# A first layer in 26 block products instead of seven, in a retention and feed-forward kernel on one core

## The chip, the cores and the metric

The kernel runs on one NeuronCore of a Trainium2 chip. The metric is the device time of one execution in microseconds (us). Before the change two runs took 679.41 and 679.5 us, median 679.45; the profiled execution spans 677.6 us.

The engines have short names in the profile: PE is TensorE (matrix products), PEld its weight loads, DVE is VectorE, ACT is ScalarE, POOL is GpSimd, SP is SyncE. PSUM is the memory into which TensorE writes, in eight banks; SBUF is the working memory.

## The reference, cut to what matters

A retention block feeds a feed-forward block. Shapes: batch 4, 8 heads, 768 positions, head size 64; so 3072 tokens of 512 numbers go into the second block, whose inner width is 2048. All is fp32.

```python
for t in range(S):
    state = gamma * state + einsum('bhd,bhe->bhde', k[:, :, t], v[:, :, t])
    y[:, :, t] = scale * einsum('bhd,bhde->bhe', q[:, :, t], state)
x = y.transpose(0, 2, 1, 3).reshape(3072, 512)

h = x @ w_in                                   # 512 -> 2048, the first layer
sp = maximum(h, 0) + log1p(exp(-abs(h)))       # softplus
g = h * erf(sp)                                # the gate
out = g @ w_out                                # 2048 -> 512, the second layer
```

## The kernel before

The first 512 tokens go through both layers by ordinary products, in four groups of inner columns, while VectorE converts the weights from 64-bit words. The other 2560 tokens go in ten chunks of 256. Each chunk is two "later groups", one for each half of the 2048 inner columns, so there are 20 later groups; I number them 0 to 19. In each, both layers are computed as seven block products in place of eight (Strassen's scheme in Winograd's form), and beside them one visit (`sub_visit`) advances the retention for a later chunk of 128 positions. There are 18 visits; the last two groups have none.

Engines run their own instructions in program order. A tile pool with `bufs=2` hands out two buffers in turn; a product into a bank has to wait until the last reader of that bank is done.

```python
ps_r = ctx.enter_context(tc.tile_pool(name="ps_r", bufs=2, space=PSUM))   # two banks
ps_h = ctx.enter_context(tc.tile_pool(name="ps_h", bufs=2, space=PSUM))   # two banks
ps_o = ctx.enter_context(tc.tile_pool(name="ps_o", bufs=1, space=PSUM))   # four banks, for the output

def sums(which, s):                  # sums of weight blocks, on VectorE, 1024 wide
    ...
    for to, a, b, plus in of:        # four for "in", four for "out", for each half s
        nc.vector.tensor_tensor(x[to], x[a], x[b], op=ALU.add if plus else ALU.subtract)
        yield

def x_sums(g):                       # sums of token blocks, once a chunk
    xs = ret.tile([P, 4, 2, P], F32, name="xs", bufs=1)
    ...
    for to, a, b in ((t1, b12, b11), (t2, b22, t1), (t3, b22, b12), (t4, b21, t2)):
        nc.vector.tensor_tensor(to, a, b, op=ALU.subtract)

def hidden_part(g, p):               # one of the seven products of the first layer
    if p == 1:
        HS[g] = act.tile([P, N], F32, name="h")
        BK[g] = [ps_h.tile([P, FG, P], F32, name="hp") for _ in range(2)]
    ...
    for u in range(FG):              # 4 x 2 = 8 matmuls of 128x128 by 128x128
        for kk in range(2):
            nc.tensor.matmul(bank[:, u, :], w_in_sb[:, s, IN[a], kk, u * P : (u + 1) * P],
                             XS[m][b][:, kk, :], ...)
    flat = bank.rearrange("p u t -> p (u t)")
    # the bank is read 512 wide: by ScalarE for p = 1, 6, 7, 4, by VectorE (added) for 2, 3, and once more for 7

def gate(g):                         # softplus and erf on ScalarE, 2048 wide
def gated(g):                        # e = h * e on VectorE, two operations of 1024
def g_sums(g):                       # four sums of blocks of g, 512 wide, on VectorE
def project_part(g, p, ...):         # one of the seven products of the second layer, 4 matmuls
    ...
    if b[0] == "T":
        need("sums out", s)          # draws weight sums until those it needs are there
    ...
    next(last_steps, None)           # draws one more step of the weight sums
def put_part(m, step):               # adds up the output and stores it, four steps

def sub_visit(j, g):
    pp = [ret_psum() for _ in range(2)]                  # both banks of ps_r
    def of_state(a):
        for u in PAIRS:
            for r in range(2):
                nc.tensor.matmul(pp[r][...], x[own, u, :], QT[j][own, u, t], ...)
    other = SC[j + 1] = [ret_psum(ps_h) for _ in range(2)]   # both banks of ps_h
    if c:
        of_state(0)
    ...

for g in range(G0, NG):              # the later groups
    hidden_part(g, 1); hidden_part(g, 2)
    ...                              # put_part of the chunk before, in every second group
    hidden_part(g, 6)
    for _ in range(2):
        next(last_steps, None)
    if not first:
        g_sums(g - 1)
    hidden_part(g, 5); hidden_part(g, 7)
    for _ in range(2):
        next(last_steps, None)
    project_part(g - 1, 1)           # in the first later group: project(g - 1, 0)
    hidden_part(g, 4); hidden_part(g, 3)
    if more: sub_visit(j, g)
    if g + 1 < NG and (g - G0) % 2: x_sums(g + 1)
    K_(j + 2); T(j + 2)              # scaling (3 operations) and transposes (2) on VectorE
    project_part(g - 1, 2); project_part(g - 1, 4)
    gate(g)
    for p in (5, 6, 7, 3): project_part(g - 1, p)
    gated(g)
```

Of the kernel before, what the change touches and what calls it, by code (L numbers as in the profile page):

```python
# [19 lines left out]
P = 128  # L20
C = 128
# [11 lines left out]
IN = {"11": 0, "12": 1, "21": 2, "22": 3, "S3": 2, "S1": 4, "S2": 5, "S4": 6}  # L33
# [6 lines left out]


# [4 lines left out]
def kernel(  # L46
# [84 lines left out]
    w_in_sb = const.tile([P, 2, 7, 2, FG * P], F32, name="w_in_sb")  # L131
    w_out_sb = const.tile([P, 2, 7, FG, DH], F32, name="w_out_sb")

    def w_in_of(ft, kk):
        half, s, i = ft // (2 * FG), ft % (2 * FG) // FG, ft % FG
        return w_in_sb[:, s, 2 * half + kk // 2, kk % 2, i * P : (i + 1) * P]

    def w_out_of(ft):
# [6 lines left out]
    spare = [  # L145
        x[:, s, 4:7].rearrange("p a b c -> p (a b c)") for s, x in
        ((0, w_out_sb), (1, w_out_sb), (1, w_in_sb), (0, w_in_sb))
    ]
    raws = [x[:, : 2 * CE].bitcast(I64) for x in spare]
    numbers = spare[0][:, 2 * CE :].bitcast(U32)  # L150
    powers = [x[:, 2 * CE :].bitcast(U32) for x in spare[1:3]]
# [38 lines left out]
    def conversion(n):  # L190
# [8 lines left out]
            range(2) if n < 4 else (None,), (slice(2), slice(2, 4)) if n == 0 else (slice(None),)  # L199
        )  # L200
        for part, rows in parts:
            last = n > 0 or rows.start == 2
            words = raws[place[n]].bitcast(U32)
            if which == "in":
                f = slice(at * 2 * P, (at + 1) * 2 * P)
                if part is not None:
                    f = slice((at * 2 + part) * P, (at * 2 + part + 1) * P)
                to = w_in_sb[:, s, 2 * half : 2 * half + 2, :, f].rearrange("p d k f -> p (d k) f")
            else:
                to = w_out_sb[:, s, 2 * half : 2 * half + 2, at * 2 : at * 2 + 2, :].rearrange(  # L210
                    "p d f c -> p d (f c)"
                )
            words = words.rearrange("p (a b w) -> p a b w", a=to.shape[1], w=2)
            number, power = (
                x.rearrange("p (a b) -> p a b", a=to.shape[1]) for x in (numbers, powers[n % 2])
            )
            if part is not None:
                f = slice(part * P, (part + 1) * P)
                words, number, power = words[:, rows, f], number[:, rows, f], power[:, rows, f]
                to = to[:, rows]  # L220
            lo, hi = words[:, :, :, 0], words[:, :, :, 1]
# [24 lines left out]

    def sums(which, s):

        if which == "in":
            assert all(("hidden", 2 * FG + s * FG + u) in done for u in range(FG))  # L250
            x = {name: w_in_sb[:, s, at] for name, at in IN.items()}
            of = (("S1", "21", "22", 1), ("S2", "S1", "11", 0), ("S3", "11", "21", 0), ("S4", "12", "S2", 0))
        else:
            assert ("project", s) in done
            x = {name: w_out_sb[:, s, at] for name, at in OUT.items()}
            of = (("T1", "12", "11", 0), ("T2", "22", "T1", 0), ("T3", "22", "12", 0), ("T4", "21", "T2", 0))
        for to, a, b, plus in of:
            nc.vector.tensor_tensor(x[to], x[a], x[b], op=ALU.add if plus else ALU.subtract)
            yield
        done.add(("sums " + which, s))  # L260
# [76 lines left out]
    state_1, state_2 = (const.tile([P, HP, D], F32, name=f"state{i}") for i in range(1, 3))  # L337
# [479 lines left out]
    XS, BK = {}, {}  # L817
# [6 lines left out]
    def x_quarter(m, dh, th):  # L824
        at = m % 2 * SCH + th * P
        return XC[m // 2][:, 2 * dh : 2 * dh + 2, at : at + P]

    def x_sums(g):

        m = chunk_of(g)  # L830
        xs = ret.tile([P, 4, 2, P], F32, name="xs", bufs=1)
        b11, b12, b21, b22 = (x_quarter(m, d, t) for d in range(2) for t in range(2))
        t1, t2, t3, t4 = (xs[:, i] for i in range(4))
        for to, a, b in ((t1, b12, b11), (t2, b22, t1), (t3, b22, b12), (t4, b21, t2)):
            nc.vector.tensor_tensor(to, a, b, op=ALU.subtract)
        XS[m] = {"11": b11, "21": b21, "22": b22, "T1": t1, "T2": t2, "T3": t3, "T4": t4}

    def hidden_part(g, p):


        m, s = chunk_of(g), (g - G0) % 2
        if p == 1:
            HS[g] = act.tile([P, N], F32, name="h")
            BK[g] = [ps_h.tile([P, FG, P], F32, name="hp") for _ in range(2)]
        h = {name: HS[g][:, i * TCH : (i + 1) * TCH] for name, i in HQ.items()}
        a, b = PRODUCTS[p]
        if a[0] == "S":
            need("sums in", s)
        bank = BK[g][0 if p in (1, 6, 7, 4) else 1]
        for u in range(FG):  # L850
            for kk in range(2):
                nc.tensor.matmul(  # L852
                    bank[:, u, :],
                    w_in_sb[:, s, IN[a], kk, u * P : (u + 1) * P],
                    XS[m][b][:, kk, :],
                    start=(p in (1, 2, 5) and u == 0 and kk == 0),
                    stop=True,
                    skip_group_check=True,
                )
        pace(1.5)  # L860
        flat = bank.rearrange("p u t -> p (u t)")
        if p == 1:
            nc.scalar.copy(h["11"], flat)
        elif p == 2:
            nc.vector.tensor_tensor(h["11"], h["11"], flat, op=ALU.add)  # L865
            pace(-0.6)
        elif p == 6:
            nc.scalar.copy(h["12"], flat)  # L868
        elif p == 7:
            nc.scalar.copy(h["22"], flat)  # L870
            other = BK[g][1].rearrange("p u t -> p (u t)")
            nc.vector.tensor_tensor(h["22"], h["22"], other, op=ALU.add)  # L872
            pace(-0.6)
        elif p == 4:
            nc.scalar.copy(h["21"], flat)  # L875
        elif p == 3:
            nc.vector.tensor_tensor(h["12"], h["12"], flat, op=ALU.add)  # L877
            pace(-0.6)
# [18 lines left out]
    def g_sums(g):  # L897
# [4 lines left out]
        for i in range(4):  # L902
            x[f"S{i + 1}"] = HS[g][:, i * TCH : (i + 1) * TCH]
        for to, a, b, plus in (
# [3 lines left out]
        G[g] = x  # L908
        pace(-2.4)
# [161 lines left out]

    j = JPC + 2
    put = None
    for g in range(G0, NG):
        first = g == G0
        more = j < NJ
        hidden_part(g, 1)
        hidden_part(g, 2)
        if first:
            gated(g - 1)  # L1080
        if put is not None:
            for step in range(3):
                put_part(put, step)
        hidden_part(g, 6)
# [3 lines left out]
        for _ in range(2):  # L1088
            next(last_steps, None)
        if put is not None:  # L1090
            put_part(put, 3)
            put = None
        if not first:
            g_sums(g - 1)
        hidden_part(g, 5)
        hidden_part(g, 7)
        for _ in range(2):
            next(last_steps, None)
        if first:
            K_(j + 1)  # L1100
            T(j + 1)
            project(g - 1, 0)
# [93 lines left out]
```

## Time and profile before

| | before |
|---|---|
| time, median of two runs | 679.45 us |
| span of the profiled execution | 677.6 us |
| TensorE matmuls, busy | 671.8 us, 6400 records |
| VectorE, busy | 392.1 us |
| ScalarE, busy | 257.0 us |
| first layer of the later groups (line 852) | 2240 records, 149.7 + 113.7 us |
| second layer of the later groups (line 924) | 1128 records, 142.0 + 112.1 us |
| granted TensorE clock | 1.000 |

How to read it: the page of the profile gives for each engine the time in which it was busy and its share of the span. A matmul of the source in fp32 shows as two records, so 20 groups of 56 matmuls are 2240 records. Records of matmuls overlap and their ends are modelled, so the distance from one start to the next tells more than the length of one record. In the lists, "h<-h,hp 128x512" means that a 512-wide operation wrote tile h from tiles h and hp; "[3.99 <-PE hp L852]" means that its engine stood idle for 3.99 us before it and that a matmul of line 852 ended the wait. V is used below for the moment at which a visit ends on TensorE.

### The profile page before, as it was taken

How to read it: one execution, taken by the hardware profiler on the slowest of the kernel's cores; microseconds unless marked ns; L12 is line 12 of the kernel's file. 1: busy time of each engine (PE TensorE's matmuls, PEld its weight loads, DVE VectorE, ACT ScalarE, POOL GpSimd, SP SyncE). 2: the span in 40 equal slices, each digit the busy share in tenths (PEclk: the TensorE clock that was granted, in tenths of full speed). 3: DMA queues.
4: the chain of work that ended last, by engine and by line, in shares of the span. 5: the costliest groups of instructions: out<-in, count | busy, mean ns of one | idle time of the engine just before them, and what ended most of it. 6: DMA issues, size and time to landing. Idle time of an engine off the chain costs nothing.

```text
span 677.6 us, 14849 instructions
## 1 busy us (share of the span) xinstructions
PE 671.8 (99%) x6400; PEld 575.4 (85%) x6400; DVE 392.1 (58%) x635; ACT 257.0 (38%) x294; POOL 7.4 (1%) x20
## 2 busy tenths in 40 slices
PE   8999999999999999999999999999999999999998
PEld 7744444668999999999999999999999999999997
DVE  5999999667845445634644553554554544333324
ACT  3477453333414415334144143242341441432430
POOL 1000000200000000000000000000000000000000
PEclk9999999999999999999999999999999999999999
DMA  9999753333423112312322321222222300000000
GB/s 188 231 254 256 178 144 77 59 61 62 119 48 75 34 32 47 76 36 43 76 41 38 76 46 31 64 44 47 69 40 45 74 2 1 1 33 1 1 32 31
DMA packets 156721, 47.67 MB, mean 70 GB/s; under 512 B 143088, under 2 KB 147568, under 8 KB 156656
## 3 DMA queue, kind: packets, MB, share of 16 engines
q1 hardware_dynamic: 156240, 46.72, 31.6%
q8 instruction: 50, 0.82, 0.5%
q14 instruction: 15, 0.12, 0.1%
q10 hardware_dynamic: 416, 0.01, 0.0%
HBM read 40.39 MB, written 6.29 MB: 69 GB/s over the span
## 4 chain that ended last, share of the span: by engine, by line
PE 98%; DMA 1%; DVE 0%; SPq 0%; ACT 0%; issue 0%
PE hp L852 37%; PE o L924 36%; PE hp L759 8%; PE o L795 8%; PE r L638 2%; PE hp L530 1%; PE o L674 1%; DMA kq<-in_k_dram 1%; PE hp L653 1%; PE r L459 1%; PE r L653 1%; PE o L506 1%; PE r L446 1%; PE r L674 0%; PE o L515 0%; PE o L499 0%
## 5 line engine op out<-in xcount | busy, mean ns | idle before, releaser
L852 PE MATMUL hp<-xs,w_in_sb 128*128 128x128 f32 x1280 | 149.7, 275 | 0.0
L852 PEld LDWEIGHTS hp<-xs,w_in_sb 128*128 128x128 f32 x1280 | 147.8, 192 | 1.5 <-issue 0.5
L924 PE MATMUL o<-w_out_sb,h 128*128 128x256 f32 (+1 forms) x648 | 142.0, 377 | 0.4 <-DVE r L1151 0.4
L924 PEld LDWEIGHTS o<-w_out_sb,h 128*128 128x128 f32 x648 | 122.3, 190 | 16.8 <-DVE r L1151 0.6
L852 PE MATMUL hp<-xT,w_in_sb 128*128 128x128 f32 x960 | 113.7, 275 | 0.0
L852 PEld LDWEIGHTS hp<-xT,w_in_sb 128*128 128x128 f32 x960 | 112.0, 192 | 1.9 <-issue 1.0
L924 PE MATMUL o<-w_out_sb,e 128*128 128x256 f32 x480 | 112.1, 383 | 0.0
L748 DVE TENSOR_TENSOR e<-h,e 128x1024 f32<-128x1024 f32 x42 | 49.5, 1221 | 100.0 <-ACT e L729 100.0
L924 PEld LDWEIGHTS o<-w_out_sb,e 128*128 128x128 f32 x480 | 88.3, 190 | 11.4
L759 PE MATMUL hp<-xT,w_in_sb 128*128 128x512 f32 (+2 forms) x144 | 56.5, 548 | 0.0
L877 DVE TENSOR_TENSOR h<-h,hp 128x512 f32<-128x512 f32 x20 | 13.8, 688 | 72.3 <-PE hp L852 72.3
L719 ACT ACT_TABLE_LOAD x24 | 30.8, 1283 | 60.8 <-issue 45.4
L759 PEld LDWEIGHTS hp<-xT,w_in_sb 128*128 128x128 f32 x144 | 25.8, 190 | 26.9 <-issue 24.6
L729 ACT ACTIVATE e<-e 128x2048 f32<-128x2048 f32 (+1 forms) x23 | 42.1, 1836 | 0.2
L719 ACT ACTIVATE e<-h 128x2048 f32<-128x2048 f32 x22 | 42.0, 1910 | 0.2
L865 DVE TENSOR_TENSOR h<-h,hp 128x512 f32<-128x512 f32 x20 | 13.7, 687 | 37.5 <-PE hp L852 37.5
L870 ACT COPY h<-hp 128x512 f32<-128x512 f32 x20 | 11.7, 586 | 61.0 <-PE hp L852 61.0
L875 ACT COPY h<-hp 128x512 f32<-128x512 f32 x20 | 11.7, 585 | 60.3 <-PE hp L852 60.3
L868 ACT COPY h<-hp 128x512 f32<-128x512 f32 x20 | 11.7, 585 | 57.1 <-PE hp L852 57.1
L692 ACT COPY xT<-r 128x256 f32<-128x256 f32 x33 | 10.8, 375 | 57.9 <-PE r L638 57.9
L729 ACT ACT_TABLE_LOAD x24 | 30.8, 1283 | 0.4
L872 DVE TENSOR_TENSOR h<-h,hp 128x512 f32<-128x512 f32 x20 | 13.8, 688 | 27.8 <-ACT h L870 27.8
(144 smaller groups left out, 667.8 us busy)
## 6 DMA issues: line engine op xcount, KB each, us to landing
w_out_sb<-in_moe_w_out_dram SPq DMA_DIRECT2D x14, 512.0 KB, 5.5
kq<-in_k_dram SPq DMA_DIRECT2D x23, 256.0 KB, 3.9
v<-in_v_dram SPq DMA_DIRECT2D x23, 256.0 KB, 3.2
out_dram<-r SPq DMA_DIRECT2D x23, 256.0 KB, 2.7
kq<-in_q_dram SPq DMA_DIRECT2D x288, 16.0 KB, 1.8
kb<-in_k_dram SPq DMA_DIRECT2D x288, 16.0 KB, 1.7
w_in_sb<-in_moe_w_in_dram SPq DMA_DIRECT2D x8, 512.0 KB, 9.5
w_in_sb<-in_moe_w_in_dram SPq DMA_DIRECT2D x8, 256.0 KB, 7.7
```

Of the source, the lines that this page charges most:

```text
L638: nc.tensor.matmul(pp[r][col * D : (col + 1) * D, u % 2, t], x[own, u, :], QT[j][own, u, t], start=first(r, col), stop=True, skip_group_ch ...
L653: nc.tensor.matmul(other[a][own, u % 2, D:] if crossed else pp[a][own, u % 2, t], V[j][t, 2 * u + r, :], AM[j][t, r, u, :D], start=crossed ...
L719: nc.scalar.activation(E[g], HS[g], AF.Softplus)
L729: nc.scalar.activation(E[g][:, half], E[g][:, half], AF.Erf)
L748: nc.vector.tensor_tensor(E[g][:, half], HS[g][:, half], E[g][:, half], op=ALU.mult)
L759: nc.tensor.matmul(HP_[ft][:, t], w_in_of(ft, kk), XC[0][:, kk, t], start=(kk == 0), stop=(kk == n_k - 1),)
L795: nc.tensor.matmul(O[0][tt].rearrange("p (d c) -> p d c", d=2), E[g][:, u * TCH + tt * P : u * TCH + (tt + 1) * P], w_out_of(ft), start=(f ...
L852: nc.tensor.matmul(bank[:, u, :], w_in_sb[:, s, IN[a], kk, u * P : (u + 1) * P], XS[m][b][:, kk, :], start=(p in (1, 2, 5) and u == 0 and ...
L865: nc.vector.tensor_tensor(h["11"], h["11"], flat, op=ALU.add)
L872: nc.vector.tensor_tensor(h["22"], h["22"], other, op=ALU.add)
L877: nc.vector.tensor_tensor(h["12"], h["12"], flat, op=ALU.add)
L924: nc.tensor.matmul(O[m][i][:, half, at], G[g][a][:, u * P : (u + 1) * P], w_out_sb[:, s, OUT[b], u, at], start=i not in started, stop=(s = ...
```

## The change

The first layer of the later groups is split finer. For each half of the inner columns the weights are cut into 4 x 4 blocks (four blocks of 128 inputs, four of 256 inner columns), the tokens into two blocks of 128. By the ordinary scheme this takes 32 products of one weight block with one token block, by seven 2x2x2 products the equal of 28; a table in the new kernel gives 26. Each takes two matmuls. What it is for: fewer matmuls on TensorE.

Each product is a step: it is added into one of four banks (two of ps_h, two of ps_r), and the running content of the bank is then read into, or added to or taken from, one or two of the eight output blocks, each 256 wide. The first write of a block is ScalarE's, the others VectorE's. The sums of blocks that the products need are 30 of weights (256 wide, for each half) and 18 of tokens (128 wide, for each chunk), most of them in place. Three projection parts of the second layer move in between the steps.

The diff, cut to its core:

```diff
+N_W, N_X = 26, 18
+W_SUMS = (
+    (16, 2, 6, "+"),
+    (2, 2, 3, "+"),
 ... 30 entries: to, a, b, sign
+X_SUMS = (
+    (0, (1, 0), (1, 1), "-"),
 ... 18 entries
+STEPS = (                    # weight block, token block, bank, new chain, reads
+    (20, 5, 0, True, ((1, False),)),
+    (21, (1, 0), 1, True, ((4, True),)),
 ... banks of steps 1 to 26: 0 1 2 3 0 1 0 1 2 3 0 1 2 3 0 1 1 1 0 2 3 1 1 0 1 3
+    (7, 13, 0, False, ((2, True),)),              # step 15
 ...
+    (13, (2, 0), 3, False, ((6, True),)),         # step 26
+)
-    w_in_sb = const.tile([P, 2, 7, 2, FG * P], F32, name="w_in_sb")
+    w_in_sb = const.tile([P, 2, N_W, 2 * P], F32, name="w_in_sb")
 ... the conversion of the weights follows the new layout
+    def sum_in(s, upto):
+        while in_sums[s] < upto:
+            to, a, b, sign = (x if i == 3 else w_in_sb[:, s, x] for i, x in enumerate(W_SUMS[in_sums[s]]))
+            nc.vector.tensor_tensor(to, a, b, op=OP[sign])
+            in_sums[s] += 1
     def sums(which, s):
         if which == "in":
-            ... four sums, 1024 wide
+            for n in range(4, 17, 4):
+                sum_in(s, n)
+                yield
+            return
 ...
-    state_1, state_2 = (const.tile([P, HP, D], F32, name=f"state{i}") for i in range(1, 3))
+    state_1 = const.tile([P, HP, D], F32, name="state1")
+    state_2 = loads.tile([P, HP * C], F32, name="kb", bufs=2)[:, : HP * D]
 ...
-        xs = ret.tile([P, 4, 2, P], F32, name="xs", bufs=1)
+        xs = ret.tile([P, N_X, P], F32, name="xs", bufs=1)
 ...
-    def hidden_part(g, p):
+    def hidden_steps(g):
+        banks = [pool.tile([P, FG, P], F32, name=name) for pool, name in ((ps_h, "hp"), (ps_r, "r")) for _ in range(2)]
+        for w, x, bank, first, reads in STEPS:
+            sum_in(s, max([n for n, of in enumerate(W_SUMS, start=1) if of[0] == w], default=0))
+            to = banks[bank]
+            for u in range(2):
+                nc.tensor.matmul(to[:, u, :], w_in_sb[:, s, w, u * P : (u + 1) * P], XS[m](x),
+                                 start=first and u == 0, stop=True, skip_group_check=True)
+            of = to[:, :2].rearrange("p u t -> p (u t)")
+            for o, plus in reads:
+                h = h_block(g, o)
+                if o in written:
+                    nc.vector.tensor_tensor(h, h, of, op=ALU.add if plus else ALU.subtract)
+                elif plus:
+                    nc.scalar.copy(h, of)
+                else:
+                    nc.scalar.activation(h, of, AF.Copy, scale=-1.0)
+                written.add(o)
+            yield
 ...
     for g in range(G0, NG):
-        ... hidden_part 1, 2, 6, 5, 7, 4, 3, with put_part, sums and project_part 1 in between
+        if first:
+            sub_begin(j)
+            sub_states(j)
+        elif put is not None:
+            put_part(put, 0)
+        more_sums = iter(()) if first else g_sums(g - 1)
+        for n, _ in enumerate(hidden_steps(g), start=1):
+            if first:
+                if n == 2:
+                    gated(g - 1)
+                elif n == 12:
+                    K_(j + 1)
+                    T(j + 1)
+                    project(g - 1, 0)
+                continue
+            if n in (3, 5, 8) and put is not None:
+                put_part(put, {3: 1, 5: 2, 8: 3}[n])
+            if n in (6, 8, 15, 16):
+                next(more_sums)
+            if n in (6, 17, 23):
+                project_part(g - 1, {6: 1, 17: 2, 23: 4}[n])
 ...
-            for p in (2, 4):
-                project_part(g - 1, p)
             gate(g)
             for p in (5, 6, 7, 3):
                 project_part(g - 1, p)
```

The visit itself is not changed.

## The prediction

> **What bounds the kernel now.** I read the busy shares and the chain of waits first, then the timeline of TensorE over one later group, then VectorE's timeline, and last the end of the run, where TensorE can be seen waiting for VectorE.
>
> ```profile
> PE 671.8 (99%) x6400; PEld 575.4 (85%) x6400; DVE 392.1 (58%) x635; ACT 257.0 (38%) x294; POOL 7.4 (1%) x20
> ...
> PE 98%; DMA 1%; DVE 0%; SPq 0%; ACT 0%; issue 0%
> PE hp L852 37%; PE o L924 36%; PE hp L759 8%; PE o L795 8%; PE r L638 2%; PE hp L530 1%; PE o L674 1%; DMA kq<-in_k_dram 1%; PE hp L653 1%; PE r L459 1%; PE r L653 1%; PE o L506 1%; PE r L446 1%; PE r L674 0%; PE o L515 0%; PE o L499 0%
> ```
>
> 98% of the chain is TensorE, and the line that the change replaces (L852) is its largest entry. So a matmul taken away is worth its full time, and every wait put before a matmul costs its full time: TensorE has no slack to absorb one. VectorE, at 58%, has slack on the average only.
>
> TensorE over one later group (start, length, engine, line, what):
>
> ```profile
> 184.03 3.73 PE L852 MATMUL hp<-xT,w_in_sb 128*128 128x128 f32 x32
> 187.60 5.52 PE L852 MATMUL hp<-xs,w_in_sb 128*128 128x128 f32 x48
> 192.96 1.89 PE L924 MATMUL o<-w_out_sb,e 128*128 128x256 f32 x8
> 194.69 1.95 PE L852 MATMUL hp<-xs,w_in_sb 128*128 128x128 f32 x16
> 196.47 1.95 PE L852 MATMUL hp<-xT,w_in_sb 128*128 128x128 f32 x16
> 198.35 0.46 PE L638 MATMUL r<-qT,state 64*64 64x64 f32 x16
> ...
> 200.38 3.72 PE L924 MATMUL o<-w_out_sb,e 128*128 128x256 f32 x16
> 203.94 7.07 PE L924 MATMUL o<-w_out_sb,h 128*128 128x256 f32 x32
> ...
> 210.84 3.73 PE L852 MATMUL hp<-xT,w_in_sb 128*128 128x128 f32 x32
> ```
>
> The group is 210.84 - 184.03 = 26.81 us and has no hole: each start follows the last one's matmuls. From starts: L852 costs (187.60 - 184.03)/32 = 0.1116 us, and each matmul of the source is two of these. One projection part (8 records) costs 194.69 - 192.96 = 1.73. The visit of the retention runs from 198.35 to 200.38, 2.03.
>
> VectorE, by width:
>
> ```profile
> 228.53 0.42 DVE L835 TENSOR_TENSOR xs<-xT 128x256 f32<-128x256 f32 x1
> 228.98 0.43 DVE L835 TENSOR_TENSOR xs<-xT,xs 128x256 f32<-128x256 f32 x1
> 229.32 0.42 DVE L835 TENSOR_TENSOR xs<-xT 128x256 f32<-128x256 f32 x1
> ```
>
> A 256-wide operation takes 0.42 to finish; the next starts after 0.34, or after 0.45 if it needs the result. In the same way the timeline gives 0.60 for 512, 1.16 for 1024, and 0.225 (0.32 dependent) for 128.
>
> What a wait costs, at the end of the run:
>
> ```profile
> 672.20 1.05 PE L924 MATMUL o<-w_out_sb,h 128*128 128x128 f32 x8
> ...
> 673.30 0.29 DVE L1151 TENSOR_TENSOR r<-r,o 128x128 f32<-128x128 f32 x1 [0.47 <-PE o L924]
> 673.64 1.16 PE L924 MATMUL o<-w_out_sb,h 128*128 128x128 f32 x8 [0.38 <-DVE r L1151]
> ```
>
> Eight matmuls at 0.1116 would end at 673.09; VectorE starts at 673.30 and TensorE returns at 673.64. So TensorE to VectorE is about 0.2 us, VectorE's own time 0.29, and back 0.05. With a 256-wide read a wait is 0.2 + 0.42 + 0.05, about **0.65 us**.
>
> [...] one L852 record shows 275 ns while starts are 111.6 apart; I count starts. [...]
>
> **The change, part by part.** I number the 26 products as steps and the later groups 0 to 19.
>
> *Removed.* A group has 7 x 8 = 56 matmuls before, 26 x 2 = 52 after: 4 x 2 x 0.1116 = 0.89 us. Twenty groups: **-17.9 us**. A step takes 4 x 0.1116 = 0.446.
>
> *VectorE's added work.* Of 26 reads of the banks, 8 are first writes by ScalarE and 18 are VectorE's: 18 x 0.34 = 6.1 us a group in place of 3 x 0.60 = 1.8. The sums of x become 18 of 128 wide, 14 x 0.225 + 4 x 0.32 = 4.4 in place of 1.5, each second group. The average share rises from 58% to some 75%: not the bound, so the sum alone costs nothing. Order and waits decide.
>
> *Steady waits.* A step may write its bank again only after the last read. The three projection parts that the change moves in between cover the closest pairs (steps 6 to 8, 17 to 18, 23 to 25). Not covered: step 26 ends the group in a bank of the pool ps_r, VectorE reads it, and the visit that follows takes both ps_r banks at once. In the order of the built program the visit's second matmul waits for VectorE. Before, ps_r was free there. 18 visits x about 0.6 = **+10.8**. Next, groups after sums of x: from the visit's end V, sums run V+1.3 to 5.7, scaling and transposes (3.1) to V+8.8, and the first half of gating ends at V+10.0; part 1, now after step 6, is due at V + 4 x 1.73 + 6 x 0.446 = V+9.6. 0.3 to 0.4 x 8 = **+2.7**. In the other groups the output sums and the G sums stand among the reads and delay the read of step 10, which step 14 needs: about 0.3 x 10 = **+3**. The steady part is then -17.9 + 16.5 = **-1.4**: nearly a draw.
>
> *Weight sums, once.* There were four of 1024 wide per half, spread long ahead. Now 30 of 256 per half, and the built order shows 14 of the first half and all 30 of the second within the steps that use them. A stall is 0.2 for the way, 0.34 per bank read in front, the sums, and 0.05.
>
> Group 0, its start:
>
> ```profile
> 125.59 0.66 DVE L439 STREAM_TRANSPOSE qT<-kq 128x512 f32<-128x512 f32 x1
> 131.30 0.69 DVE L865 TENSOR_TENSOR h<-h,hp 128x512 f32<-128x512 f32 x1 [5.04 <-PE hp L852]
> ...
> 127.46 3.73 PE L852 MATMUL hp<-xT,w_in_sb 128*128 128x128 f32 x32
> ```
>
> VectorE was done 1.2 us before TensorE began. It now has 16 early sums (6.2 for 4.7) and the sums of x (4.4 for 1.5) more, so it ends near 130.7; the masks and the state that free the ps_r banks end near 131.8, while TensorE, after 1.1 of scores (132.91 to 133.99 before) and two steps, wants one at 129.4: 2.4. Gating then delays step 8 by 0.4. Sums inside: step 12, one sum, 1.0; step 15, five, 0.2 + 0.34 + 1.9 + 0.05 = 2.5; step 18, no projection part between, 0.65; step 20, one, 1.0; step 22, two reads and three sums, 2.0; steps 24 and 26, two dependent sums, 1.45 each. Together 2.8 + 10.1 = **+12.9**.
>
> Group 1: its first product needs eight sums, which stand behind gating. ScalarE's gate (two table loads of 1.28 and two passes of 1.91) takes 6.4 and ends at V+7.3, gating at V+9.6, the chained sums at V+13.0; TensorE is there at V + 3 x 3.45 = V+10.4: 2.6. Steps 7 and 12: 0.2 + 1.3. Steps 15, 20, 22, 26: 2.5 + 1.0 + 2.0 + 1.45. Before part 4, placed after step 23, the T sums of the second layer are now all drawn at once: four of 1.16 that the part needs, 0.2 + 0.34 + 4.7 + 0.05 = 5.3, and two more before the sums of step 24: 1.5. Together **+17.8**.
>
> The sum: 679.45 - 1.4 + 12.9 + 17.8 = 708.8. I put **708 us**, a little less, since waits that follow closely let VectorE catch up.
>
> **Rivals.** (a) *The count decides:* VectorE keeps ahead, waits are hidden, only -17.9 remains: 661.5 us, or about 664 with part of the first groups' cost. For it: the projection parts are placed with care where banks repeat, and VectorE has 42% idle. Against it: the built order puts sums directly ahead of the products that need them, and the visit behind the last read. (b) *Draw:* the weight sums hide behind TensorE's queue of work in groups 0 and 1, and only the steady waits remain: 678 us. Against it: TensorE works in order, so it can't pass a product whose weight is missing. (c) *VectorE becomes the bound throughout:* each of its 18 reads lags and holds the next step, one or two us more in each group: 720 to 735. Against it: between step 26 and the next step 6 it has some 12 us, in which its other work of about 9 fits.
>
> **Range and chances.** The count is sure to 1 us. The visit's wait could be 0.4 to 0.8 (7 to 14 us); the other steady waits 0 to 10; the two first groups 22 to 38. These don't all err one way: **697 to 717** holds 8 in 10. More than 2% slower means above 693; to stay under it, half of the first groups' waits would have to vanish. Within 2% 0.08, faster by 2% 0.03, slower 0.89.
>
> **What would show it.** The count: 2080 records of the new product line in place of 2240, 0.1116 apart. The visit: a hole of 0.6 us in each of 18 groups, put down to VectorE. A steady pair of groups of some 2 x 26.7 us, against 2 x 26.81. Group 0 about 13 and group 1 about 17 us longer than the steady ones' change, with TensorE waiting for the weight sums (L347) and, once, over 5 us for the T sums (L360). I am wrong if groups 0 and 1 have no such holes (then 678), if the visit goes on without one (then near 698), or if holes stand before most steps of the steady groups (then over 717).

## The result, and the profile after

The changed kernel takes **743.25 us** (median; 742.46 to 744.03) against 679.45 before: a ratio of 1.0938, with a 95% interval of 1.0907 to 1.097. The prediction was 708 us with a range to 717. The direction was right and the size was half: 63.8 us were lost, 28.6 were foreseen.

From the page of the changed kernel (busy time and share of TensorE; the granted clock in 40 slices; the chain of work by engine):

```profile
PE 684.6 (92%) x6240; PEld 574.5 (77%) x6240; DVE 528.8 (71%) x1127; ACT 265.3 (36%) x374; POOL 7.8 (1%) x20
...
PEclk9999999986797999999999999999999999999999
...
PE 72%; DVE 10%; SPq 6%; DMA 6%; ACT 4%; issue 2%; DVEq 0%
```

160 records are gone, as the count of products says (6400 to 6240). Yet TensorE's share of the chain fell from 98% to 72%, and 26% went to VectorE, DMA queues, DMA and ScalarE: holes. The row of the clock has four digits below 9, all from the ninth to the thirteenth slice (148 to 241 us). So the slowed clock lies in one stretch and not throughout; the waits of the next list show a second stretch of loss, before it.

Its waits (who waits <- for whom: us in total, times, longest):

```profile
PE hp L959 <- DVE w_in_sb L347: 12.6, 8, 2.4
DVE w_in_sb L315 <- DMA w_in_sb<-in_moe_w_in_dram: 12.4, 2, 7.1
...
PE r L634 <- DVE qT L543: 5.6, 1, 5.6
...
PE hp L863 <- ACT h L881: 5.4, 2, 4.8
PE o L1023 <- DVE w_out_sb L360: 5.2, 1, 5.2
...
PE r L742 <- DVE h L971: 3.9, 15, 0.3
```

L959 are the new products, L347 the weight sums, L360 the T sums, L742 the visit: those waits were foreseen. L315 (the weights' conversion) and L863 (the first layer of the first 512 tokens) are not lines that the change was meant to touch, and L634 (the retention's scores) it only moves ahead of group 0's first product. Those three waits are the news.

I place the loss with four marks in both timelines of TensorE: the start of the third block (of four) of the first 512 tokens' second layer, its end, the start of the last projection block of group 0, and the start of the last projection block of group 1. All are times in us.

| stretch | before | after | lost | foreseen |
|---|---|---|---|---|
| start to the second layer's third block | 113.7 | 135.4 | 21.6 | 0 |
| from its end to the last project block of group 0 | 19.3 | 43.6 | 24.3 | 12.0 |
| from there through group 1 | 30.4 | 51.9 | 21.5 | 16.9 |
| the other 18 groups, to the end | 500.5 | 497.75 | -2.7 | 0.4 |

(The third block itself takes 13.7 in both. The rows add up to 64.7, the difference of the two profiled spans; the medians differ by 63.8.) The foreseen numbers are the prediction's 12.9 and 17.8 less 0.89 for each group's count, and its -1.4 without the first two groups' count. The last row is the steady part. The last step of a later group, the visit, and the next projection there:

```profile
270.31 0.61 PE L959 MATMUL r<-xT,w_in_sb 128*128 128x128 f32 x4
...
271.43 0.40 PE L742 MATMUL r<-qT,state 64*64 64x64 f32 x11 [0.26 <-DVE h L971]
...
273.45 7.17 PE L1023 MATMUL o<-w_out_sb,h 128*128 128x256 f32 x32
```

From the end of the step (270.31 + 0.446) to 273.45 are 2.69 us, where the visit took 2.03 before: 0.66 of wait, in each group with a visit. (The bracket has 0.26 of it; up to its modelled end, the record before counts as busy.) Two groups in a row take 26.69 and 26.63 in place of 26.81 and 26.73.

### The profile page after: what moved, and what is told of

Read it like the earlier page. It is cut to its first block, busy times and chain, and to the rows that moved or that the text cites. A ratio compares the mean times of both kernels' runs of the same rounds, so it can differ in the third digit from the quotient of the medians.

```text
span 742.3 us, 15275 instructions
## 1 busy us (share of the span) xinstructions
PE 684.6 (92%) x6240; PEld 574.5 (77%) x6240; DVE 528.8 (71%) x1127; ACT 265.3 (36%) x374; POOL 7.8 (1%) x20
## 4 chain that ended last, share of the span: by engine, by line
PE 72%; DVE 10%; SPq 6%; DMA 6%; ACT 4%; issue 2%; DVEq 0%
PE o L1023 32%; PE hp L959 21%; PE r L959 11%; SPq L187 3%; DMA w_in_sb<-in_moe_w_in_dram 3%; PE o L899 2%; DVE h L971 2%; PE r L742 2%; DVE w_in_sb L347 1%; SPq L266 1%; DMA kq<-in_q_dram 1%; PE hp L634 1%; SPq L209 1%; DVE w_out_sb L360 1%; DMA w_out_sb<-in_moe_w_in_dram 1%
## 5 line engine op out<-in xcount | busy, mean ns | idle before, releaser
L959 PE MATMUL hp<-xs,w_in_sb 128*128 128x128 f32 x1040 | 147.5, 281 | 14.1 <-DVE w_in_sb L347 11.3
L971 DVE TENSOR_TENSOR h<-h,hp 128x256 f32<-128x256 f32 x240 | 98.7, 419 | 78.9 <-PE hp L959 74.7
L959 PEld LDWEIGHTS hp<-xs,w_in_sb 128*128 128x128 f32 x1040 | 136.8, 195 | 20.2 <-DVE w_in_sb L347 12.2
L852 DVE TENSOR_TENSOR e<-h,e 128x1024 f32<-128x1024 f32 x42 | 49.3, 1214 | 37.9 <-ACT e L833 37.9
L863 PE MATMUL hp<-xT,w_in_sb 128*128 128x512 f32 (+2 forms) x144 | 60.7, 576 | 10.4 <-ACT h L881 5.4
L959 PE MATMUL r<-xs,w_in_sb 128*128 128x128 f32 x480 | 68.2, 279 | 2.0 <-DVE w_in_sb L347 2.0
L959 PEld LDWEIGHTS r<-xs,w_in_sb 128*128 128x128 f32 x480 | 61.5, 196 | 2.9 <-issue 2.9
L973 ACT COPY h<-r 128x256 f32<-128x256 f32 x80 | 27.8, 375 | 99.9 <-PE r L959 99.9
L971 DVE TENSOR_TENSOR h<-h,r 128x256 f32<-128x256 f32 x120 | 48.6, 419 | 14.6 <-PE r L959 10.9
L863 PEld LDWEIGHTS hp<-xT,w_in_sb 128*128 128x128 f32 x144 | 26.7, 198 | 40.7 <-issue 31.6
L959 PE MATMUL hp<-xT,w_in_sb 128*128 128x128 f32 x320 | 50.5, 282 | 1.3 <-DVE w_in_sb L347 1.3
L959 PEld LDWEIGHTS hp<-xT,w_in_sb 128*128 128x128 f32 x320 | 45.0, 197 | 2.8 <-DVE w_in_sb L347 1.6
L959 PE MATMUL r<-xT,w_in_sb 128*128 128x128 f32 x240 | 38.2, 282 | 2.6 <-DVE w_in_sb L347 2.6
L823 ACT ACT_TABLE_LOAD x24 | 30.8, 1283 | 19.3 <-DVE h L971 18.9
L959 PEld LDWEIGHTS r<-xT,w_in_sb 128*128 128x128 f32 x240 | 32.0, 194 | 3.5 <-DVE w_in_sb L347 3.1
```

The costliest lines, as they stand in the source:

```text
L823: nc.scalar.activation(E[g], HS[g], AF.Softplus)
L852: nc.vector.tensor_tensor(E[g][:, half], HS[g][:, half], E[g][:, half], op=ALU.mult)
L863: nc.tensor.matmul(HP_[ft][:, t], w_in_of(ft, kk), XC[0][:, kk, t], start=(kk == 0), stop=(kk == n_k - 1),)
L959: nc.tensor.matmul(to[:, u, :], w_in_sb[:, s, w, u * P : (u + 1) * P], XS[m](x), start=first and u == 0, stop=True, skip_group_check=True,)
L971: nc.vector.tensor_tensor(h, h, of, op=ALU.add if plus else ALU.subtract)
L973: nc.scalar.copy(h, of)
```

## The experiments

### The stage that the change was not meant to touch

Before, the odd pieces of the weights' conversion used free space of `w_in_sb` for a scratch. The new blocks 16 to 25 take that space, and the change puts the scratch into the last two blocks, across both halves s. VectorE in the changed kernel (start, length, what; in brackets the idle time ahead and what ended it), and TensorE behind it:

```profile
33.55 0.43 DVE L315 TENSOR_SCALAR w_in_sb<-w_out_sb 128x512 uint32<-128x512 uint32 x1 [5.28 <-DMA w_in_sb<-in_moe_w_in_dram]
...
52.03 0.43 DVE L315 TENSOR_SCALAR w_in_sb<-w_in_sb 128x512 uint32<-128x512 uint32 x1 [7.14 <-DMA w_in_sb<-in_moe_w_in_dram]
```

```profile
36.52 15.67 PE L863 MATMUL hp<-xT,w_in_sb 128*128 128x512 f32 x32 [4.60 <-DVE w_in_sb L333]
...
56.97 5.40 PE L863 MATMUL hp<-xT,w_in_sb 128*128 128x512 f32 x8 [4.78 <-ACT h L881]
```

The operation that writes the scratch waits for loads that don't go to the scratch. A view over both halves starts in half 0, ends in half 1, and spans blocks 16 to 23 of half 1, where raw weights land; in the order of the built program the first such write of L315 waits for six DMA semaphores in place of two. That the span of the view is why is inferred; that the place is the cause, the next two runs show. ScalarE's next instruction waits behind it (5.97 and 6.55 us in the changed kernel), and with it a copy that frees TensorE's bank.

**e1: the scratch alone goes elsewhere**, into the buffer of the x sums, which is not yet in use.

```diff
-        w_in_sb[:, :, 24:26].rearrange("p h a f -> p h (a f)").bitcast(U32),
+        halves(ret.tile([P, N_X, P], F32, name="xs", bufs=1)[:, :8].rearrange("p a f -> p (a f)")),
```

> The changed kernel with one thing moved: the scratch of the odd weight conversions, which the change laid across both halves of the weight tile, is given a place of its own (the buffer of the token sums, idle then). Theory A (the stage before group 0 is 21.6 us longer because that scratch, by its span from the first half to the second, is taken to overlap the landing place of raw weights, so that its writes wait for loads that have nothing to do with them): the waits of the conversions on loads vanish (5.3 and 7.1 us), the second-layer products ahead of group 0 start near 114 us in place of 135, and the time falls by 18 to 24 us, to about 721. Rival B (the new layout of the weights, its access patterns or the larger token sums slow the conversions themselves): the same operations keep their later place and the time stays within 5 us of 743.

Measured: 721.59 us, ratio 1.0609 (1.0585 to 1.0632), 21.7 below the changed kernel. The third block starts at 113.99 again.

**e2: the kernel before, with only its odd scratch in such a straddling place.**

```diff
+            if n % 2 and n < n_p - 1:
+                power = w_in_sb[:, :, 6, 1, :].bitcast(U32)      # both halves s
...
```

> The kernel before with that part alone: the scratch of the odd conversions laid across both halves of the weight tile, as two pieces of 512, all else as before. Theory A: the same waits appear, the second-layer products ahead of group 0 start some 15 to 22 us later than 113.7, and the time rises from 679.5 to between 694 and 702. Rival B (it is the layout of the weights or the new sums that slow the stage): within 3 us of 679.5.

Measured: 703.71 us, ratio 1.0355 (1.034 to 1.0371), 24.2 us lost, a little over what was expected. The two waits are there, and the third block starts at 137.50:

```profile
33.41 0.43 DVE L229 TENSOR_SCALAR w_in_sb<-w_out_sb 128x512 uint32<-128x512 uint32 x1 [4.98 <-DMA w_in_sb<-in_moe_w_in_dram]
...
53.95 0.43 DVE L229 TENSOR_SCALAR w_in_sb<-w_in_sb 128x512 uint32<-128x512 uint32 x1 [8.24 <-DMA w_in_sb<-in_moe_w_in_dram]
```

Nothing else of the change is in this kernel. So a third of the whole loss is the place of a scratch, shown from both sides.

### The wait ahead of the visit

**e3: the pools of the banks change places**, so that step 26, the last, ends in a ps_h bank.

```diff
-        banks = [... for pool, name in ((ps_h, "hp"), (ps_r, "r")) for _ in range(2)]
+        banks = [... for pool, name in ((ps_r, "r"), (ps_h, "hp")) for _ in range(2)]
```

> The changed kernel with the two pools of the four banks exchanged: steps on banks 0 and 1 use ps_r, steps on banks 2 and 3 use ps_h, so that the last step's bank is not one that the visit takes first. Theory: a visit is 2.69 us from the last step's end to the first projection part, 2.03 before, and the 0.66 is the wait for the last read; with the exchange only the read of step 25 is left to wait for, which has had one step of 0.45 to run, so the visit shrinks to about 2.25 and the time by 18 x 0.4 = 7 us, to about 736. Rival (the 0.66 is not that wait but slower matmuls of the visit, or the same wait then comes at the visit's second pair of banks): less than 2 us gained.

Measured: 738.38 us, ratio 1.0862 (1.0835 to 1.0889). The periods fall to 26.24 and 26.19, 0.44 less, and no wait of L742 is left in its list. From the last block of group 1 to the end the trace is 6.5 us shorter (491.28 for 497.75). The total fell by 4.9, not 7: the first later group began 2.5 us later than in the changed kernel. Of this, 1.5 stood before it (the third block starts at 136.85 in place of 135.35), and 0.90 is a wait that the exchange itself brings, since the first step now takes a ps_r bank that the scores have just used:

```profile
159.25 1.20 PE L959 MATMUL r<-xs,w_in_sb 128*128 128x128 f32 x4 [0.90 <-PE r L654]
```

So 0.44 of the 0.66 is the visit's wait for a ps_r bank, and removing it costs 0.9 us once.

### The sums inside the first two groups

**e4: no weight sum inside a step.** The products use one of the 16 original blocks in place of a sum, and the sums that steps would draw are left out; those that run ahead, and all products, are kept.

```diff
-            sum_in(s, max([n for n, of in enumerate(W_SUMS, start=1) if of[0] == w], default=0))
...
-                    w_in_sb[:, s, w, u * P : (u + 1) * P],
+                    w_in_sb[:, s, w % 16, u * P : (u + 1) * P],
```

> The changed kernel without the weight sums inside the steps; the steps take weight blocks that are there instead, so what it computes leaves out 14 sums of the first half and 30 less those still drawn elsewhere of the second. Theory (group 0 and 1 wait for these sums, and the idling also halves the granted clock for part of them): group 0 falls from 43.6 us to some 25, group 1 from 38.6 to some 28 (the four T sums ahead of part 4 stay), the clock stays at 1.000 but for that one wait, and the time falls by 25 to 32 us, to about 714. Rival (VectorE is simply full in these two groups, and its reads of the banks hold TensorE even without the sums): less than 15 us.

Measured: 720.12 us, ratio 1.0597 (1.057 to 1.0624); 23.1 less, below the expected 25. All waits on L347 are gone, and the wait ahead of group 1's first product too. The profile names ScalarE's copy (L914) for that one; since it goes with the sums, it was theirs. But the wait for the T sums, 5.2 us, became 8.5: TensorE came to it earlier. The run takes the sums' work from VectorE along with their waits, so it doesn't tell the two apart; e6 will.

**e7: e1 with the T sums drawn one by one** at steps 6 to 20 of group 1, in place of all at part 4.

```diff
-        for which, n in (("in", 1), ("out", 0), ("out", 1)):
+        for which, n in (("out", 0), ("out", 1)):
...
+            if n in (11, 14, 20):
+                next(last_steps, None)
```

> The changed kernel with the scratch in its own place (721.6) and one thing more: the T sums of the second layer are drawn one by one after steps 6, 11, 14, 17 and 20 of group 1 in place of six in a row ahead of part 4. Theory: the wait of 5.2 us ahead of part 4, the halved clock after it and the 1.5 us at step 24 go, while single T sums delay a read by 1.2 here and there: 6 to 9 us gained, to about 714. Rival (VectorE only moves the same work about and a later step waits as long): within 2 us of 721.6.

Measured: 719.86 us, ratio 1.0586 (1.0565 to 1.0607), 1.7 below e1 where 7 were hoped for, and not clear of the spread of e1's runs (718.41 to 722.14). In its waits the 5.2 us ahead of part 4 are gone, and the waits for weight sums ahead of products into ps_h banks grew from 12.9 us in e1 (8 times, longest 2.4) to

```profile
PE hp L959 <- DVE w_in_sb L347: 17.5, 9, 3.6
```

So the work moved and the wait with it. Is VectorE then simply full in these groups? Its timeline in e1, group 0, says no:

```profile
145.60 2.00 DVE L347 TENSOR_TENSOR w_in_sb<-w_in_sb 128x256 f32<-128x256 f32 x5
148.41 0.42 DVE L971 TENSOR_TENSOR h<-h,hp 128x256 f32<-128x256 f32 x1 [0.80 <-PE hp L959]
149.97 0.42 DVE L971 TENSOR_TENSOR h<-h,hp 128x256 f32<-128x256 f32 x1 [1.14 <-PE hp L959]
...
159.66 0.42 DVE L971 TENSOR_TENSOR h<-h,hp 128x256 f32<-128x256 f32 x1 [2.17 <-PE hp L959]
```

L971 reads a bank and waits for TensorE; L347 stands behind such reads; the next product waits for L347. The two engines take turns. If that is the whole of it, it is the order of the work that costs, while both have time; e6 tests this.

### Does it help to order it otherwise?

**e5: e1 with e3's pools, all 60 weight sums on GpSimd, well ahead** (five tiny scale operations go to VectorE instead, and the T sums are spread as in e7).

```diff
-            nc.vector.tensor_tensor(to, a, b, op=OP[sign])
+            nc.gpsimd.tensor_tensor(to, a, b, op=OP[sign])
...
```

> The changed kernel with its causes mended together: scratch in its own place, pools exchanged, all 60 weight sums given to the idle GpSimd as soon as their half is converted (the small scaling products that GpSimd did go to VectorE), the T sums spread over steps 6 to 20. Theory (the waits for weight sums, with the scratch and the visit, are the whole loss): groups 0 and 1 fall to some 23 and 28 us, the clock stays at 1.000, and the time falls to between 664 and 676, below the kernel before. Rival (GpSimd is too slow for 60 sums of 256, above 1.2 us each[...]): the steps wait for it, and the time stays above 690.

Measured: 692.3 us, ratio 1.0183 (1.0167 to 1.0198): 29.3 less than e1, but above the 690 that the rival named. GpSimd's own work is one line:

```profile
92.40 66.74 POOL L347 TENSOR_TENSOR w_in_sb<-w_in_sb 128x256 f32<-128x256 f32 x60 [85.54 <-DVE xs L327]
```

1.11 us a sum on the mean, against some 0.40 on VectorE. And VectorE itself slows down meanwhile. The same two conversions in e5, while GpSimd runs, and then in e6, where it doesn't:

```profile
98.31 1.75 DVE L327 SCALAR_TENSOR_TENSOR w_out_sb<-w_out_sb 128x1024 uint32<-128x1024 uint32 x1
100.09 1.63 DVE L333 SCALAR_TENSOR_TENSOR w_out_sb<-w_out_sb 128x1024 f32<-128x1024 f32 x1
```

```profile
97.09 1.22 DVE L327 SCALAR_TENSOR_TENSOR w_out_sb<-w_out_sb 128x1024 uint32<-128x1024 uint32 x1
98.35 1.23 DVE L333 SCALAR_TENSOR_TENSOR w_out_sb<-w_out_sb 128x1024 f32<-128x1024 f32 x1
```

A third to 43% longer. So VectorE is hindered while GpSimd works, and not in every operation alike: sums of two SBUF blocks mostly grow by about 0.5 us whatever their width (128x128 from 0.28 to 0.81, 128x512 from 0.68 to 1.22), one-input conversions (L319) from 0.69 to 1.10, the transposes, 0.70 and 0.66, not at all. What hinders them, these lengths don't tell. VectorE's transposes came late, and TensorE's scores with them:

```profile
143.71 1.13 PE L632 MATMUL r<-qT,kT 64*64 64x64 f32 x32 [16.15 <-DVE qT L541]
```

The first step came at 146.69, where before the change it was 127.46, and 132.81 in e1: 13.9 us of what the steps gained were lost ahead of them.

**e6: as e5, but with the sums in one go on VectorE** (the scale operations stay on GpSimd), the last 14 of half 0 after step 2 of group 0, the 30 of half 1 in group 0's tail.

```diff
                 if n == 2:
                     gated(g - 1)
+                    sum_in(0, len(W_SUMS))
...
             gate(g)
+            sum_in(1, len(W_SUMS))
```

> The same without GpSimd: VectorE makes the last 14 sums of the first half in one go after step 2 of group 0, the 30 of the second half in one go in the tail of group 0, T sums spread. Theory (each sum cost a way there and back and a slowed clock, not its VectorE time; made in one go they cost TensorE one wait of some 5 us in group 0 and one of 5 to 8 in group 1): the time is 721.6 - 5 (pools) - 15 to 22, so between 693 and 702. Rival (VectorE is full in these two groups whatever the order): above 708.

Measured: 688.14 us, ratio 1.0117 (1.01 to 1.0133), better than expected: 33.5 less than e1. Pools (6.5 us in e3's steady part) and spread T sums (1.7 in e7) are in it; the rest, over 20 us, is order: as many sums, on the same engine. A row of sums costs one wait, 2.53 us behind the 14 and 3.21 behind the 30, not one for each step.

### What the waits cost beyond their length

**e10: e1 with the x sums of the first chunk behind the scores** in VectorE's order.

```diff
-            ([], [(x_sums, G0)]),
+            ([], []),
...
             sub_states(j)
+            x_sums(g)
```

> The changed kernel with the scratch in its own place (721.6 us) with one difference: the 18 x sums of the first chunk stand after the scores and the state sums of the first later group on VectorE, not before its transposes. In that run the scores waited 3.2 us for the transposes and the first step began 5.3 us later than before the change. Theory (the step of the prediction that failed is the place of the scores: VectorE's 4.1 us of x sums stand ahead of the transposes, and the wait for them also halves the clock for the first steps): the wait falls away, the first step begins 2 to 4 us earlier, 717 to 719.5. Rival (VectorE is the bound of this stretch, in whatever order): the first step waits for its x sums instead, 720.5 to 723.

Measured: 719.12 us, ratio 1.0574 (1.0524 to 1.0625), too near e1 to tell apart by time. The trace tells: the scores ran at 127.77 without a wait, but the first step came at 131.36, only 1.45 us earlier, after a hole that the profile puts to no engine. TensorE, and VectorE's sixth x sum, which makes the token block of that step (X_SUMS has it as number 5):

```profile
131.36 1.19 PE L959 MATMUL hp<-xs,w_in_sb 128*128 128x128 f32 x4 [2.44 <-issue]
```

```profile
130.98 0.28 DVE L940 TENSOR_TENSOR xs<-xs 128x128 f32<-128x128 f32 x1
```

So the step waits for its x sums instead, as the rival said, and the last block of group 1 begins only 0.6 us earlier than in e1. My theory fell. It isn't shown that no order helps: VectorE's x sums run from 129.97 to 134.1, and just ahead of them it stood idle for 2.18 us, waiting for the scores.

**e11: e1 with its waits filled.** Products of a token block and zeros are added to a bank ahead of the steps that wait, 40 in group 0 and 54 in group 1. They change no sum.

```diff
+            if g < G0 + 2 and step != 23:
+                fill(to, m, FILL[s].get(step, 0))   # {12: 3, 15: 10, 18: 4, 20: 8, 22: 5, 24: 5, 26: 5} in group 0
...
```

> The changed kernel with the scratch in its own place (721.6 us), with products of a token block and a block of zeros added to a bank ahead of the steps that wait in the first two later groups: 40 products in the first and 54 in the second, each group of them sized at 0.22 us a product to just fit in the wait that the trace shows (0.85 us at step 12, 2.44 at step 15, 1.0, 2.0, 1.3, 1.3, 1.3, and 4.4 of the 5.2 us ahead of part 4). They change no sum. Theory (about 10 of the lost microseconds are not the waits but the halved clock after them): TensorE stays busy, its clock stays up from step 12 on, and 4 to 9 us come back though work was added: 712 to 718. Rival (the clock falls for another reason, or the waits are bound by TensorE's own part of the round trip): 720 to 726.

Measured: 717.12 us, ratio 1.0558 (1.0532 to 1.0584): 4.5 less than e1 by the medians, whose intervals lie end to end; in the traces the last block of group 1 begins 5.8 us earlier (216.86 for 222.66). The stretch from 150 to 160 us (length, then busy time of PE, PEld, DVE, ACT, POOL, and the granted clock), in e1 and then in e11:

```profile
150.00:160.00 10.00, 6.20 (x24) 5.34 (x24) 4.18 (x11) 0.00 (x0) 0.00 (x0) 0.50 0.18 36
```

```profile
150.00:160.00 10.00, 8.87 (x76) 8.49 (x76) 4.87 (x13) 0.00 (x0) 0.00 (x0) 1.00 0.17 34
```

More products, and less time. TensorE still has to wait for VectorE's sums, now behind products of zeros, and its clock no longer falls there: the granted clock of whole executions was 0.992 to 0.995 in e11's four runs and 0.972 to 0.979 in e1's. But the waits alone do not fix when the clock falls. The waits of steps 15 to 20 (2.44, 0.58 and 1.01) are the same in e7 without any filling. The 8 records behind each took 1.35, 2.08 and 2.04 us in e1, the last two in the stretch at 0.50, and 1.16, 1.16 and 1.13 in e7, where the next step of 4 to take 1.22 came at 157.64. In e3 the 8 records took 1.13 to 1.16 behind all of 2.44, 0.58, 1.01 and 2.05, and a step of 4 took 1.22 at 185.62. From the records' lengths in the changed kernel (a step of 4 records takes 1.22 in place of 0.61, a part 3.78 in place of 1.89) I estimate some 7 us in group 0 and 3 to 4 in group 1 as halved clock; e11 brings back about half of that, since the holes ahead of group 0 and of group 1 are not filled.

### A version that pays

**e8: e6, with the first two later groups in plain form**: products of the untouched blocks, 64 records of 256 wide or the time of 128 of a step's, in place of 104, so that no weight sum is due before group 2; the x sums of the first chunk are left out, the T sums stand in group 0.

```diff
-        for n, _ in enumerate(hidden_steps(g), start=1):
+        for n, _ in enumerate(plain_steps(g) if g < G0 + 2 else hidden_steps(g), start=1):
...
```

> The run with the sums ahead on VectorE (688.1 us), changed so that the first two later groups compute their hidden layer without any weight sums: 128 records each from the untouched weight blocks, in place of 104. No weight sum is then needed before the third later group: the 30 of half 0 are made in the first group's tail and the second group, the 30 of half 1 in the second group's tail and the third group, the T sums during the first group's steps, and the 18 x sums of the first chunk are left out. Theory (the whole loss before the third later group is the stock of VectorE work that must be done before a product can start, and the wait and the halved clock that follow from it): each of the two groups costs 16 records x 0.1116 = 1.8 us more than before the change and nothing else, the blocks of the steady part begin near 177.1 + 3.6 = 180.7 us, and the rest takes the 493.0 us that the run with the sums ahead shows from there: 673.7; with up to 5 us of waits in the third group from the sums moved into it: 673 to 679. Rival (the first two groups are slow because a chain in four banks with ScalarE and VectorE reads is slower in them, or because the late sums only move the wait to the third group): 682 or more.

Measured: 687.88 us, ratio 1.0139 (1.0115 to 1.0162): the rival's number, for another reason. TensorE, and then VectorE between the two places:

```profile
167.11 3.38 PE L1047 MATMUL o<-w_out_sb,e 128*128 128x256 f32 x8 [4.56 <-DVE e L850]
...
201.71 3.62 PE L1047 MATMUL o<-w_out_sb,e 128*128 128x256 f32 x8 [4.87 <-DVE e L850]
```

```profile
185.91 0.42 DVE L781 TENSOR_TENSOR state<-state,o 128x256 f32<-128x256 f32 x1 [13.15 <-PE r L776]
```

I had put 24 sums, and then 12, ahead of the gate's product L850, and left VectorE idle for 13 us between. Both parts behind those waits are slow as well: 3.38 and 3.62, where the next ones (176.21 and 211.08) take 1.89.

**e9: the same work in the gaps.** Ten sums ahead of the gate, 20 in the steps of group 1, then 14 sums of half 1 there as TensorE leaves the blocks that they overwrite, 16 in group 2; the scores behind half of group 0's products.

```diff
+            if g == G0 + 1 and 3 < n < 14:
+                sum_in(0, 10 + 2 * (n - 3))
+            if g == G0 + 1 and n > 13:
+                sum_in(1, min((n - 13) * 2, 9) if n < 21 else min(n - 11, 14))
+            if g == G0 + 2 and 2 < n < 19:
+                sum_in(1, 12 + n)
...
```

> The run with two groups in plain form (687.9 us) with the same work in other places: only 10 sums of half 0 stand before the gate's product in the first group's tail, the other 20 in the second group's steps; 14 sums of half 1 follow there as soon as TensorE has read the blocks that they overwrite, and 16 in the third group's steps, none before a gate's product; the scores of the first group come after 16 of its 32 matrix products. That trace showed TensorE waiting 4.6 and 4.9 us on the gate's product L850 behind 25 and 12 sums, and VectorE idle for 13.2 us in between. Theory (what is lost is the waits and the halved clock behind them, not the amount of VectorE work): both waits and the 2 us ahead of the first step fall away, and the third group loses 1 to 2 us to its 16 sums: 673 to 677, faster than before the change for the first time. Rival (VectorE has not the room: the sums only delay the reads of the third group): 681 or more.

Measured: **674.51 us**, ratio 0.9928 (0.9915 to 0.9942): faster than the kernel before, by 0.7%. From its page, and its list of waits:

```profile
PE 664.6 (98%) x6160; PEld 561.1 (83%) x6160; DVE 507.9 (75%) x1073; ACT 265.1 (39%) x374; POOL 4.7 (1%) x20
...
PEclk9999999999999999999999999999999999999999
```

```profile
PE o L1047 <- DVE e L850: 1.3, 1, 1.3
PE r L957 <- DVE h L969: 1.0, 1, 1.0
```

No clock digit is below 9, and no wait in the later groups is over 1.3 us. (6160 records in place of 6240: a plain group has 64 of 256 wide, where a group of steps has 104 of 128.) The last block of group 1 starts at 183.16, against 177.12 before and 244.55 in the changed kernel. No run tells how the 13.4 us gained on e8 divide between the places of the sums and that of the scores.

## Why the prediction was wrong, point by point

- **The count, -17.9:** right. 2080 records of the new line in 20 groups, a step at 0.446.
- **The visit's wait, 0.6:** right, 0.66; e3 removes 0.44 of it.
- **The other steady waits, 5.7 in sum:** half. Eighteen groups were to cost 0.4 us and gained 2.7; with 18 x 0.89 for the count and 16 x 0.66 for the visits this leaves about 2.8. Of this, 1.9 is a single wait for gating (L852) in group 2, where eight were foreseen.
- **The sums' waits in group 0:** right in size. Foreseen for steps 12, 15, 18, 20, 22, 24, 26: 1.0, 2.5, 0.65, 1.0, 2.0, 1.45, 1.45. In the changed kernel:

```profile
172.05 1.16 PE L959 MATMUL hp<-xs,w_in_sb 128*128 128x128 f32 x8 [2.44 <-DVE w_in_sb L347]
174.44 2.08 PE L959 MATMUL hp<-xs,w_in_sb 128*128 128x128 f32 x8 [0.58 <-DVE h L971]
177.53 2.05 PE L959 MATMUL r<-xs,w_in_sb 128*128 128x128 f32 x8 [1.01 <-DVE w_in_sb L347]
181.55 2.07 PE L959 MATMUL hp<-xs,w_in_sb 128*128 128x128 f32 x8 [1.97 <-DVE w_in_sb L347]
```

  with 0.85 for step 12 and 1.31 for each of the last two: 9.5 in all for 10.1. The way of counting a wait (to VectorE, its operations, and back) holds here.
- **The T sums ahead of part 4, 5.3:** right, 5.2.
- **The step that failed first: what the change touches.** The prediction began its sum at group 0 and took all before as unchanged. The diff shows the scratch moved, and I passed over it. The built order, which I used for the sums, shows six waits in place of two on L315. That is 21.7 us (e1) of the 35 by which the prediction was short; the first two groups are 17 more, mostly the next two points, which share the slow scores of group 0, and the steady part gives 3 back.
- **The second: the halved clock was not priced.** The prediction adds the waits at their bare length. The lines above show it: 2.05 to 2.08 for 8 records, in place of 1.06, and the granted clock was 0.67 from 170 to 180 us and 0.50 from 180 to 190. Some 10 us by the estimate above, of which e11 shows about 5 by giving TensorE other work. The waits in those lines are of 0.6 to 2.4 us, some 2 us apart; e3 and e7 show that the same waits need not bring it at once.
- **The third: the start of group 0, 2.8.** I let the scores run before VectorE's transposes were done; they need them (5.6 us of wait on L543, 3.2 in e1), and the first step came 7.7 us after the projection, 5.1 in e1, with no such hole before. In e10 VectorE serves the scores first, and the step comes only 1.45 us earlier. Without the 1.1 us of the scores themselves the term measured 4.0 in e1 and 6.6 in the changed kernel in place of 2.8. The end of VectorE's work was reckoned about right for e1 (130.7; the last transpose ends at 130.97), but the wait for it stood earlier in TensorE's order, ahead of the scores and not behind them, and the scores then ran slow (1.7 us in e1, 1.9 in the changed kernel).
- **The rivals:** (a) and (b) fell with the waits in groups 0 and 1. (c), VectorE as the bound throughout, comes nearest by number (720 to 735) and is wrong by mechanism: in the steady groups nothing of it shows, and even in group 0 VectorE waits for TensorE.

Open stays what decides when the clock falls, and so how the halved clock divides between the two groups to better than a microsecond or two: with the same waits in group 0, from the first step to the last projection block, e1 took 35.8 us for it and e7 33.4.

## What to carry to other kernels

Before counting a change's operations, compare the waits of every instruction of the old and new program, those that the change only displaces too: a strided scratch across two halves of a buffer can wait for all that lies between (24.2 us lost in e2, 21.7 won back in e1). Where two engines hand work to and fro in order, put a row of preparation into a gap of the preparing engine, or start with a plain form that needs none: against the kernel before, the last block of group 1 comes some 45 us late with the sums inside the steps (e1, 222.66 against 177.12), 18 with them in rows ahead (e6, 195.16), and 6 with them in the gaps and two plain groups (e9, 183.16). And price a wait of a microsecond that comes again and again at its length plus the slower work after it (in the changed kernel 2.05 to 2.08 us for 8 records in place of 1.06).

## What the runs showed of the hardware that was not expected

- TensorE's granted clock fell to 0.50 over a stretch in which no single wait was over 2.5 us and TensorE was busy 62% (e1, 150 to 160); with zero products in the waits it stayed at 1.00 (e11). With the same three waits (2.44, 0.58, 1.01) and no filling, the 8 records behind each took 1.13 to 1.16 us in e7 and 1.35 to 2.08 in e1.
- Sixty 128x256 fp32 sums took GpSimd 1.11 us each on the mean, beside a busy VectorE; VectorE takes some 0.40. While GpSimd worked through them (e5), most of VectorE's operations with two SBUF inputs grew by about 0.4 to 0.5 us whatever their width: 128x1024 conversions took 1.63 to 1.75 us in place of 1.22, 128x128 sums up to 0.81 in place of 0.28; its transposes (0.70) did not.
